# An S4 convolution and gated FFN, forward and backward: the order of the last forward convolution, the gates and the first backward convolution

## The chip, the cores and the metric

The kernel runs on one core of a Trainium2 chip. A time is device microseconds of one execution. Twelve runs of the kernel before gave a median of 740.47 us (737.26 to 746.09). One execution was also recorded by the profiler; every engine instruction, wait and transfer quoted below is of that one.

## What is computed

Input `x` is 2048 x 512 in bf16. A layer norm gives `xn`. Two branches read it. Branch A is a long causal convolution along the rows, one filter for each of the 512 channels, whose filters are built from complex exponentials (S4), plus a skip term. Branch B is a feed-forward net, `silu(xn @ w1) @ w2`, with w1 512 x 1792. The output multiplies A with a gate made of B:

```python
x = A_u
xn = _layernorm(x, axis=-1)
s = _A_ref(xn, A_A_re, A_A_im, A_B_re, A_B_im, A_C_re, A_C_im, A_log_dt, A_Dskip)
g = _silu(_B_ref(xn, B_w1, B_w2))
return x + s * g
```

The kernel returns this output and, for a given `grad_out`, the gradients with respect to x, the eight S4 parameters, w1 and w2. With o the result of the feed-forward net, the gradient that flows into branch A is `d s = grad_out * silu(o)`; the one that flows into branch B is `d o = grad_out * s * silu'(o)`.

## The kernel before, in words

The 2048 rows lie as 128 partitions x 16 row groups (t), the channels as 4 blocks of 128 (b). The work falls into stages.

**Forward.** `gen_tables` makes the filter of a block, `gen_conv_x` the spectrum of xn, `gen_conv_fwd` the convolution. A convolution is a transform in two TensorE steps with a transpose by DMA between them (`dft_fwd`, L276 to L300: matmuls L286, evacuations L287 by ScalarE, two transposes L288, matmuls L297 and L298, evacuations L299), a complex product on VectorE in two halves (`cplx_mul`, L323 to L337), and an inverse transform (`dft_inv`, L303 to L320: matmuls L310, evacuation L312, matmuls L319, and a `consume`). The evacuations have the line L44 or L45 in the profile, those of the helper `Evac` (A is ScalarE, D is VectorE). For the forward convolution `consume` adds the skip term and writes the block's result `S_b` (L518, L519). Beside this runs `gen_ffn_fwd` (hidden products L541, output products L558, result `ob`, stored to `Od`). At its end w1 and, later, w2 are turned on TensorE (L118), and each group of eight turned blocks is copied from PSUM back over the weight (tile W), by ScalarE and VectorE in turn (`evw`, pattern "AD", L1022).

**Gates.** `gen_gate_rows` (L569 to L604) goes through the rows in 8 chunks of two row groups. A chunk reads o, takes silu (tile g, three buffers, L593) and tanh (into the row store `do`, which the profile calls YD, L594) on ScalarE, writes `ds` on VectorE (L595), and makes d o with two operations on GpSimd (L597, L598) and four on VectorE (L599 to L603). L603 multiplies by the results S of blocks 0 to 2, loaded into a tile with two buffers (L589). `grad_out` is held whole in Gr, four loads of 512 KB (L576). The factor of block 3 comes last, when its convolution is done (L1101).

**Backward.** `gen_conv_bwd` needs all of `ds` for its first transform (L286 on ds), and then runs two inverse transforms for each block, one for the filter's gradient (dK) and one for the input's (du, L664 and L665). `gen_ffn_da` turns d o (doT), multiplies it with turned w2 (L886, ps_da), evacuates this on VectorE times the slope of silu (L888; the slope itself is two ScalarE and three VectorE operations for each half chunk, L875, L876 and L108 to L110), and multiplies with turned w1 (L897, ps_dx). `gen_out` makes the output. Then `gen_ssm_bwd` runs the gradient of the filter parameters, with `gen_ffn_da` and later the weight gradients (`gen_dw2`, `gen_dw1`) as TensorE work beside it; the weight gradient of w1 is the last.

**What sets the order.** The generators emit work in turns (`interleave`, `paced`, `woven`); the framework then orders the instructions of each engine by its own schedule, so that order of emission and order on an engine differ in places. [...]All plain loads and the DMA transposes of this part are issued by SyncE (SP), also in order: a load that waits for a buffer holds back all that stand behind it. PSUM tiles come from three pools: pf (3 buffers: feed-forward products, turned blocks), pc (2: transforms) and pt.

The part at issue, before:

```python
    interleave([gen_conv_fwd(k, 3), ffn, gates], [1, 3, 1])
```

then block 3's factor, the turning of w2, four steps of the backward convolution, and `paced(bwd, woven([ffb, out], [2, 1]), BR)`.

Of the kernel before, what the change touches and what calls it, by code (L numbers as in the profile page):

```python
# [10 lines left out]
ACT = mybir.ActivationFunctionType  # L11
ALU = mybir.AluOpType
F32 = mybir.dt.float32
BF16 = mybir.dt.bfloat16
# [3 lines left out]
P = 128  # L18
# [1 line left out]
PB = 18  # L20


BR, SR = 1.7, 0.5

E_EXP = [256 * i for i in range(1, 9)] + list(range(8)) + [258, 260, 262, 516, 772]
Y_EXP = [8 * j for j in range(1, 8)] + [64, 128, 192]
# [21 lines left out]
def interleave(gens, weights=None):  # L48
    gens = list(gens)
    weights = list(weights or [1] * len(gens))  # L50
    alive = [True] * len(gens)
    while any(alive):
        for i, g in enumerate(gens):
            if not alive[i]:
                continue
            for _ in range(weights[i]):
                try:
                    next(g)
                except StopIteration:
                    alive[i] = False  # L60
                    break
# [34 lines left out]
def paced(gen, other, rate):  # L96

    n = 0.0
    for _ in gen:
        n += rate  # L100
        while n >= 1:
            next(other, None)
            n -= 1
# [462 lines left out]

def gen_gate_rows(k, gp, lag):  # L569

    nc = k.nc
    TT = nc.vector.tensor_tensor
    last = k.T // 2
    Gr = gp.tile([P, k.T, k.D], BF16, name="Gr")
    for t in range(0, k.T, 4):
        nc.sync.dma_start(Gr[:, t:t + 4, :], k.g_v[:, t:t + 4, :])  # L576
    for c in range(last):
        while k.rows_done <= c or (c not in k.ob and k.rows_done < min(c + 1 + lag, last)):
            yield
        ts = slice(2 * c, 2 * c + 2)  # L580
        o = k.do[:, ts, :]
        src = o
        if c in k.ob:
            src = k.ob.pop(c)[:]
        else:
            nc.sync.dma_start(o, k.Od[:, ts, :])
        G = Gr[:, ts, :]
        S = gp.tile([P, 3, 2, P], BF16, name="S", tag="S", bufs=2)
        nc.sync.dma_start(S[:].rearrange("p b t d -> p b (t d)"), k.Sd[0:3, :, 256 * c:256 * c + 256].rearrange("b p n -> p b n"))  # L589
        if src is o:  # L590
            yield
        g = gp.tile([P, 2, k.D], BF16, name="g", tag="g", bufs=3)
        nc.scalar.activation(out=g[:], in_=src, func=ACT.Silu)  # L593
        nc.scalar.activation(out=o, in_=src, func=ACT.Tanh, scale=0.5)  # L594
        TT(out=k.ds[:, ts, :], in0=G, in1=g[:], op=ALU.mult)  # L595

        nc.gpsimd.tensor_scalar(out=o, in0=o, scalar1=-0.5, scalar2=0.5, op0=ALU.mult, op1=ALU.add)  # L597
        nc.gpsimd.tensor_scalar(out=g[:], in0=g[:], scalar1=1.0, scalar2=-1.0, op0=ALU.mult, op1=ALU.add)  # L598
        TT(out=o, in0=o, in1=g[:], op=ALU.mult)  # L599
        nc.vector.tensor_single_scalar(out=o, in_=o, scalar=1.0, op=ALU.add)  # L600
        TT(out=o, in0=o, in1=G, op=ALU.mult)
        o3 = o[:, :, 0:3 * P].rearrange("p t (b d) -> p b t d", b=3)
        TT(out=o3, in0=o3, in1=S[:], op=ALU.mult)  # L603
        yield  # L604


def gen_out(k, pool):
# [377 lines left out]
def kernel(ctx, tc, A_u, A_A_re, A_A_im, A_B_re, A_B_im, A_C_re, A_C_im, A_log_dt, A_Dskip, B_x, B_w1, B_w2, grad_out,  # L985
           out_0, out_1, out_2, out_3, out_4, out_5, out_6, out_7, out_8, out_9, out_10, out_11):
    nc = tc.nc
    k = KCtx()
    k.nc, k.tc = nc, tc
    k.outs = [out_0, out_1, out_2, out_3, out_4, out_5, out_6, out_7, out_8, out_9, out_10, out_11]  # L990
    L, D, F = A_u.shape[1], A_u.shape[2], B_w1.shape[1]
# [7 lines left out]
    def pool(name, side=None, es=ctx, **kw):  # L999
        kw.setdefault("bufs", 1)  # L1000
        return es.enter_context(tc.tile_pool(name=name, side=side, reuse_waits="tile", **kw))
# [17 lines left out]
    k.pc = ctx.enter_context(tc.tile_pool(name="pc", bufs=2, space=PSUM))  # L1019
    k.pt = ctx.enter_context(tc.tile_pool(name="pt", bufs=1, space=PSUM))  # L1020
    k.evk, k.evc, k.evf, k.evb, k.evv = (Evac(nc, "A") for _ in range(5))
    k.evx, k.evw = Evac(nc, "D"), Evac(nc, "AD")  # L1022

    k.st = nc.gpsimd.dma_start
    k.const = pool("const")
# [2 lines left out]
    es_f, es_x, es_t = (ctx.enter_context(ExitStack()) for _ in range(3))  # L1028
# [6 lines left out]
    with ExitStack() as es_s:  # L1035
# [6 lines left out]
        S = load_params(k, wp, 0, D, ("Ar", "Ai"))  # L1042
# [29 lines left out]
    def dft_pool(name, es, nbuf, base=None, **kw):  # L1072
        t = pool(name, es=es, **kw).tile
        return SimpleNamespace(tile=lambda shape, dt, name, tag: t(shape, dt, name=name, tag=tag, bufs=nbuf[tag]) if tag in nbuf
                               else base.tile(shape, dt, name=name, tag=tag))
# [14 lines left out]
    ffn = gen_ffn_fwd(k)  # L1090
    paced(chain(), ffn, 0.62)
    es_t.close()
    k.late = True
    k.ds = pool("ds", side="right", es=es_x).tile([P, 16, D], BF16, name="ds")
    es_g = es_x.enter_context(ExitStack())
    gates = gen_gate_rows(k, pool("gate", side="right", es=es_g), 1)

    interleave([gen_conv_fwd(k, 3), ffn, gates], [1, 3, 1])
    for t in (slice(0, 8), slice(8, 16)):
        last = k.do[:, t, 3 * P:4 * P]  # L1100
        nc.vector.tensor_tensor(out=last, in0=last, in1=k.S_b[:, t], op=ALU.mult)  # L1101
    es_f.close()
    es_g.close()
    base = dft_pool("dftb", es_x, {"cm2": 1, "xd": 1, "dD": 1, "w8b": 2}, k.dft, side="right")
    turn = itertools.cycle(["w8"] * 4 + ["w8b"] * 2)
    k.dftb = SimpleNamespace(tile=lambda shape, dt, name, tag: base.tile(shape, dt, name=name, tag=next(turn) if tag == "w8" else tag))
    da = pool("da", es=es_d)
    turned_in_place(k, k.W2, k.evw)
    bwd = gen_conv_bwd(k)
    out = gen_out(k, da)  # L1110
    for i in range(4):
        next(bwd)
    ffb = gen_ffn_da(k, da)
    paced(bwd, woven([ffb, out], [2, 1]), BR)
    es_x.close()
# [35 lines left out]
```

## Time and profile before

| what | value |
|---|---|
| median of 12 runs | 740.47 us |
| the profiled execution's own time | 740.77 us |
| its span, first to last instruction | 739.1 us |
| TensorE busy, of the span | 600.7 us (81%) |
| VectorE busy | 548.3 us (74%) |
| ScalarE busy | 506.6 us (69%) |
| GpSimd busy | 108.5 us (15%) |
| mean granted TensorE clock | 0.932 |
| chain that ended last: issue / VectorE / TensorE / DMA | 27% / 12% / 9% / 8% |

Time and span differ by 1.7 us, which lies around the program. A row of the table of windows gives, for a stretch of the span in us, how long each engine was busy in it, with the count of instructions, then the mean granted clock of TensorE (1.00 is full), the share of the DMA engines and their rate. A row of the timeline gives start and length of a merged run of instructions, its engine, line, operation and tiles; what stands in brackets is how long the engine had idled before it, and what released it. SPq and ACTq are the issuing queues.

### The profile page before, as it was taken

The page shows a single profiled execution, that of the slowest core. Times are in us where ns is not written, and L with a number is a line of the kernel's source. Part 1 is how long each engine was busy: PE and PEld are TensorE (multiplying, and loading weights), DVE is VectorE, ACT ScalarE, POOL GpSimd, SP SyncE. Part 2 cuts the span into 40 slices and gives each one's busy share as a digit, 9 for nine tenths or more (in the row PEclk, how much of TensorE's full clock was granted, in tenths as well). Part 3 has the DMA queues.
Part 4 walks back from the last instruction along what each step waited for, and adds up shares of the span by engine and source line. Part 5 has one row for each costly group of instructions (what it writes and reads, how often), then busy time and mean ns, then how long its engine had stood idle before and what let it go on. Part 6 is the DMA issues. An engine that isn't in the chain of part 4 may idle for free.

```text
span 739.1 us, 13979 instructions
## 1 busy us (share of the span) xinstructions
PE 600.7 (81%) x5459; PEld 432.0 (58%) x5500; DVE 548.3 (74%) x1086; ACT 506.6 (69%) x707; POOL 108.5 (15%) x180
## 2 busy tenths in 40 slices
PE   0667968869999955587989879978898978979995
PEld 0435645555675733454757657747576665756784
DVE  6969997869988759868698779747796677896000
ACT  7768759669799866857879587646846758882211
POOL 2172100000100034700000000000002003113210
PEclk9979989999999985789899989999999989999998
DMA  9877957679589776589988955789979999841782
GB/s 286 313 167 189 288 173 200 247 199 306 231 216 275 310 242 161 167 221 283 287 186 242 234 194 178 166 196 212 234 154 257 277 235 282 228 132 55 153 178 65
DMA packets 207042, 159.26 MB, mean 215 GB/s; under 512 B 129024, under 2 KB 185344, under 8 KB 203392
## 3 DMA queue, kind: packets, MB, share of 16 engines
q1 hardware_dynamic: 193856, 135.29, 69.3%
q0 software_dynamic: 6224, 18.10, 6.8%
q10 hardware_dynamic: 6896, 4.98, 2.1%
q8 instruction: 43, 0.70, 0.4%
q14 instruction: 23, 0.19, 0.1%
HBM read 65.14 MB, written 62.26 MB: 172 GB/s over the span
## 4 chain that ended last, share of the span: by engine, by line
issue 27%; DVE 12%; PE 9%; DMA 8%; POOL 4%; SPq 4%; ACT 2%; ACTq 0%; POOLq 0%; DVEq 0%
PE ps_da L886 2%; PE ps_dx L897 2%; DMA YT<-Yd 2%; DMA pd_l<-Pd 2%; SPq L718 2%; DVE sp_in L332 1%; SPq L346 1%; DVE Tp L739 1%; PE ps_v L729 1%; DMA out_dram<-go_x 1%; DMA Kd<-KE 1%; DVE sp_in L333 1%; DVE YD L599 1%; PE ps_i L310 1%; POOL out_dram L809 1%
## 5 line engine op out<-in xcount | busy, mean ns | idle before, releaser
L44 ACT CAST dA<-ps_s 128x1024 bf16<-128x1024 f32 x96 | 94.5, 1038 | 18.0 <-PE ps_s L298 9.6
L886 PE MATMUL ps_da<-doT,W 128*128 128x256 bf16 x448 | 62.7, 283 | 11.1 <-DVE dhT L888 7.1
L541 PE MATMUL ps_h<-XT,W 128*128 128x256 bf16 x448 | 62.5, 291 | 1.5 <-ACT hT L44 0.8
L310 PE MATMUL ps_i<-I,sp_in 128*128 128x256 bf16 x384 | 54.7, 288 | 8.5 <-DVE sp_in L333 4.2
L558 PE MATMUL ps_o<-W,aT 128*128 128x512 bf16 x209 | 54.5, 393 | 4.1 <-ACT aT L549 2.9
L886 PEld LDWEIGHTS <-W 128*128 128x128 bf16 x448 | 44.7, 102 | 21.8 <-issue 13.0
L739 DVE TENSOR_TENSOR Tp<-Vb,Eb 128x1344 bf16<-128x1344 bf16 x64 | 52.0, 853 | 6.9 <-issue 5.7
L44 ACT CAST dB<-ps_i 128x1024 bf16<-128x1024 f32 x48 | 47.1, 1019 | 12.9 <-PE ps_i L310 10.6
L897 PE MATMUL ps_dx<-W,dhT 128*128 128x512 bf16 x224 | 55.5, 388 | 0.5 <-ACT doT L44 0.5
L44 ACT CAST o<-ps_w 128x256 bf16<-128x256 f32 (+1 forms) x42 | 18.5, 442 | 50.9 <-PE ps_w L947 41.9
L541 PEld LDWEIGHTS <-W 128*128 128x128 bf16 x448 | 45.7, 104 | 12.7 <-issue 2.6
L929 PE MATMUL ps_w<-YD,a_tok 128*128 128x512 bf16 x210 | 51.3, 388 | 2.0 <-ACT o L44 1.2
L947 PE MATMUL ps_w<-dh_tok,xn 128*128 128x256 bf16 x448 | 50.5, 273 | 2.5 <-DMA dh_tok<-DHd 2.5
L310 PEld LDWEIGHTS <-sp_in 128*128 128x128 bf16 x384 | 37.7, 103 | 24.1 <-DVE sp_in L333 8.5
L888 DVE SCALAR_TENSOR_TENSOR dhT<-dhT,ps_da 128x512 bf16<-128x512 bf16 x56 | 37.5, 682 | 16.6 <-PE ps_da L886 16.2
L947 PEld LDWEIGHTS <-xn 128*128 128x128 bf16 x448 | 43.3, 98 | 8.9 <-issue 3.8
L44 ACT CAST Vb<-ps_v 128x672 bf16<-128x672 f32 x64 | 43.0, 730 | 6.7 <-PE ps_v L729 6.7
L286 PEld LDWEIGHTS <-TF 128*128 128x128 bf16 x384 | 27.0, 104 | 26.9 <-issue 15.3
L419 ACT ACTIVATE sn<-V 128x1024 bf16<-128x1024 int32 (+3 forms) x40 | 35.2, 899 | 8.8 <-DVE V L417 8.8
L729 PE MATMUL ps_v<-Gb,YT 128*128 128x168 bf16 x256 | 28.7, 243 | 14.3 <-ACT Vb L44 10.3
L297 PE MATMUL ps_s<-dB,F 128*128 128x512 bf16 x87 | 34.5, 404 | 6.9 <-DMA dB<-dA 4.2
L298 PE MATMUL ps_s<-dB,F 128*128 128x512 bf16 x95 | 36.9, 394 | 2.0 <-DMA dB<-dA 1.3
(223 smaller groups left out, 1383.5 us busy)
## 6 DMA issues: line engine op xcount, KB each, us to landing
Yd<-YD SPq DMA_DIRECT2D x8, 1024.0 KB, 5.6
sp_in<-Ud SPq DMA_DIRECT2D x8, 1024.0 KB, 7.8
h_in<-Hd SPq DMA_DIRECT2D x14, 512.0 KB, 5.1
Ed<-E SPq DMA_DIRECT2D x8, 672.0 KB, 5.1
Eb<-Ed SPq DMA_DIRECT2D x8, 672.0 KB, 5.4
Hd<-hT POOLq DMA_DIRECT2D x8, 512.0 KB, 6.1
Ud<-dA SPq DMA_DIRECT2D x4, 1024.0 KB, 9.8
KXd<-dA SPq DMA_DIRECT2D x4, 1024.0 KB, 6.3
```

The costliest lines, as they stand in the source:

```text
L44: return self.nc.scalar.copy(out=out, in_=in_)
L298: nc.tensor.matmul(out=ps[:, 4 * u:4 * u + 4], lhsT=F2[:, m1], rhs=B[:, 1, g0:g0 + 4, :], start=False, stop=True)
L310: nc.tensor.matmul(out=ps[:, g], lhsT=Y[:, c, g0 + g, :], rhs=k.I2[:, c].rearrange("p c m -> p (c m)"), start=(c == 0), stop=(c == 1))
L541: nc.tensor.matmul(out=ps[:, j], lhsT=k.W1[:, dk, ft * P:ft * P + P], rhs=XTv[:, :, dk, :], start=(dk == 0), stop=(dk == DK - 1))
L558: nc.tensor.matmul(out=ps[:], lhsT=aT[:, ft, t * P:t * P + P], rhs=k.W2[:, ft, :], start=(ft == 0), stop=(ft == FT - 1))
L729: nc.tensor.matmul(out=ps[:, u, 168 * c:168 * c + 168], lhsT=YT[:, c, q + u, :], rhs=Gb[:, q0 + q + u].rearrange("p w x -> p (w x)"), star ...
L739: k.nc.vector.tensor_tensor(out=Tp[:, c, :, r ^ c].rearrange("p e (q w) a -> p q w e a", w=2), in0=Vb[:, :, c].rearrange("p q w (e a) -> p ...
L886: nc.tensor.matmul(out=ps[:, j], lhsT=k.W2[:, ft, dk * P:dk * P + P], rhs=dTv[:, :, dk, :], start=(dk == 0), stop=(dk == DK - 1))
L888: nc.vector.scalar_tensor_tensor(out=dh[:, i0:i0 + 2, :], in0=dh[:, i0:i0 + 2, :], scalar=1.0, in1=ps[:], op0=ALU.add, op1=ALU.mult)
L897: nc.tensor.matmul(out=ps[:], lhsT=dhs[ft // 8][:, ft % 8, t * P:t * P + P], rhs=k.W1[:, :, ft * P:ft * P + P], start=(ft == 0), stop=(ft ...
L929: nc.tensor.matmul(out=ps[:], lhsT=at[:, t, :], rhs=k.do[:, t, :], start=(t == 0), stop=(t == k.T - 1))
L947: nc.tensor.matmul(out=ps[:], lhsT=k.xn[:, t, dk * P:dk * P + P], rhs=dh[:, t].rearrange("p j n -> p (j n)"), start=(t == 0), stop=(t == k ...
```

## The change

- The gates no longer run beside the last forward convolution in the order of emission. `gates` first emits the loads of three chunks; then `gen_conv_fwd(k, 3)` is emitted whole, with three steps of the feed-forward for each of its steps; then the gates, with the first backward convolution in turn with them.
- In a chunk, silu and d s come first, then tanh; d o of chunk c is emitted after d s of chunk c + 1.
- `grad_out` comes in chunks of 256 KB into a ring of four buffers instead of a whole tile.
- The backward convolution takes eight steps (EARLY) before the feed-forward backward is emitted, from the moment when all of d s is emitted; it was four. Its additional transform buffers are opened ahead of the gates.
- The turned weights are copied out of PSUM by VectorE alone (`evw` pattern "D").

```diff
-BR, SR = 1.7, 0.5
+BR, SR, EARLY = 1.7, 0.5, 8
...
-def gen_gate_rows(k, gp, lag):
+def gen_gate_rows(k, gp, ahead=3):
...
+    def load(c):
         ts = slice(2 * c, 2 * c + 2)
...
+        Gr[c] = gp.tile([P, 2, k.D], BF16, name="Gr", tag="Gr", bufs=4)
+        nc.sync.dma_start(Gr[c][:], k.g_v[:, ts, :])
+        if c < k.rows_done and c not in k.ob:
+            nc.sync.dma_start(k.do[:, ts, :], k.Od[:, ts, :])
+            held[c] = k.do[:, ts, :]
+
+    def d_s(c):
+        src = held.pop(c) if c in held else k.ob.pop(c)[:]
+        ts = slice(2 * c, 2 * c + 2)
         g = gp.tile([P, 2, k.D], BF16, name="g", tag="g", bufs=3)
         nc.scalar.activation(out=g[:], in_=src, func=ACT.Silu)
...
+        TT(out=k.ds[:, ts, :], in0=Gr[c][:], in1=g[:], op=ALU.mult)
+        nc.scalar.activation(out=k.do[:, ts, :], in_=src, func=ACT.Tanh, scale=0.5)
+        Sr[c] = gp.tile([P, 3, 2, P], BF16, name="S", tag="S", bufs=2)
...
+    for c in range(n):
...
+        g[c] = d_s(c)
+        k.ds_all = c == n - 1
+        yield
+        if c > 0:
+            d_o(c - 1, g.pop(c - 1))
+            yield
+        if c + ahead < n:
+            load(c + ahead)
+    d_o(n - 1, g.pop(n - 1))
...
-    k.evx, k.evw = Evac(nc, "D"), Evac(nc, "AD")
+    k.evx, k.evw = Evac(nc, "D"), Evac(nc, "D")
...
-    interleave([gen_conv_fwd(k, 3), ffn, gates], [1, 3, 1])
+    k.dfx = dft_pool("dfx", es_x, {"w8x": 2, "dD": 1}, k.dft, side="right")
+    turn = itertools.cycle(["w8", "w8x", "w8x", "w8", "w8", "w8"])
...
+    def early():
+        while not k.ds_all:
+            yield
+        for _ in range(EARLY):
+            next(bwd)
+            yield
+
+    next(gates)
+    paced(gen_conv_fwd(k, 3), ffn, 3)
+    interleave([gates, early()], [1, 1])
...
-    turn = itertools.cycle(["w8"] * 4 + ["w8b"] * 2)
...
+    k.dfx = dft_pool("dftb", es_x, {"cm2": 1, "xd": 1}, first, side="right")
...
-    for i in range(4):
-        next(bwd)
     ffb = gen_ffn_da(k, da)
     paced(bwd, woven([ffb, out], [2, 1]), BR)
```

The operations of d o, in `d_o`, are those of before.

## The prediction

> **What bounds the kernel now.** I read the page first: TensorE is busy 81% of the span, no other engine above 74%, and the chain that ended last spreads over all engines with no line above 2%. So no engine is the bound everywhere, and the question is which stretch is thin. The table of windows answers it:
>
> ```profile
> 270.00:280.00 10.00, 3.40 (x34) 2.95 (x32) 9.71 (x10) 5.01 (x6) 8.25 (x7) 0.65 0.50 186
> 280.00:290.00 10.00, 4.47 (x22) 2.55 (x23) 10.00 (x15) 5.38 (x7) 4.58 (x5) 0.50 0.85 189
> 290.00:300.00 10.00, 6.58 (x29) 3.27 (x28) 9.03 (x15) 9.14 (x10) 5.62 (x3) 0.67 0.56 206
> 300.00:310.00 10.00, 7.12 (x67) 5.46 (x66) 7.64 (x13) 9.47 (x10) 9.51 (x4) 0.82 0.62 184
> 310.00:320.00 10.00, 4.49 (x41) 4.16 (x41) 10.00 (x17) 6.66 (x7) 0.00 (x0) 0.66 0.39 83
> ...
> 440.00:475.00 35.00, 34.67 (x304) 24.88 (x303) 31.98 (x45) 25.00 (x26) 0.51 (x1) 1.00 0.53 167
> 475.00:490.00 15.00, 13.11 (x96) 8.46 (x95) 8.41 (x14) 7.67 (x6) 0.00 (x0) 1.00 0.84 150
> 490.00:510.00 20.00, 15.24 (x176) 12.85 (x175) 14.21 (x18) 9.29 (x15) 0.00 (x0) 0.91 0.91 227
> 510.00:530.00 20.00, 16.24 (x173) 12.49 (x172) 14.04 (x18) 17.61 (x21) 0.00 (x0) 0.91 1.11 224
> ```
>
> From 270 to 320 us TensorE (first pair) works 26.1 of 50 us at a clock of 0.50 to 0.82, while VectorE (third pair) is full in most rows: the gates. From 440 on TensorE is nearly full. The timeline shows how the gates hold block 3's convolution:
>
> ```profile
> 266.81 14.28 SPq L589 DMA_DIRECT2D S<-Sd  x3
> ...
> 270.22 2.73 DVE L595 TENSOR_TENSOR ds<-Gr,g 128x1024 bf16<-128x1024 bf16 x3 [8.11 <-DMA Gr<-in_grad_out_dram]
> ...
> 274.43 1.06 ACT L593 ACTIVATE g<-YD 128x1024 bf16<-128x1024 bf16 x1 [5.98 <-DVE YD L599]
> ...
> 281.19 4.83 SPq L288 DMA_TRANSPOSE dB<-dA  x2
> ...
> 310.58 1.21 DVE L519 TENSOR_TENSOR S_b<-ps_i,xd 128x1024 bf16<-128x1024 f32 x1
> ...
> 319.62 0.92 PE L886 MATMUL ps_da<-doT,W 128*128 128x256 bf16 x7 [2.02 <-ACT doT L44]
> ```
>
> VectorE waits 8.11 us for the gradient; so the fourth silu waits 5.98 us for a g buffer, and behind it stand the evacuations of the transform, whose matmuls were done at 269.6 (they come at 275.86). SP stands on the third S load until 281.1, and behind it stand the two transposes. Then VectorE mixes gate work into the product, whose first row (L330) comes at 293.66, and gets late to S_b. The feed-forward backward starts at 319.62.
>
> **The change, part by part.** The built order of each engine gives the sequence; durations are the trace's. Up to the inverse of block 2 (256.75) the two kernels agree.
>
> *Weights out of PSUM.* In the groups by form:
>
> ```profile
> L44 ACT COPY W<-pt_t 128x1024 bf16<-128x1024 bf16 x7 | 6.9, 1015 | 1.7 <-PE ps_i L319 1.7
> ...
> L45 DVE COPY W<-pt_t 128x1024 bf16<-128x1024 bf16 x7 | 4.8, 681 | 3.1 <-PE pt_t L118 3.1
> ```
>
> Seven copies leave ScalarE (6.9 us) and cost VectorE 4.8, about 0.6 each back to back, 4.2. [...] The rows have VectorE faster, so I take 4.2. The first four hide in VectorE's idle time from 252 to 258; the rest stand among the gates.
>
> *Gap, first half.* The new order has three Gr loads ahead of Kb's load, 0.75 MB against the 2 MB behind it before. Before, they took 5.3 us or more to land; issued at about 262 they land near 267 (bounds 265 and 270). VectorE then makes two d s, with weight copies between, 267 to 270; the weights' transposes stand ahead of Kb's matmuls, so these run at 270, later than 268.6 before. ScalarE has two ob evacuations, three silu and four tanh until 272 (nine rows of 0.6 to 1.06 us from 263.6) and no g wait in front of the transform; evacuations at 272 to 276 against 275.9 to 280.4. SP has only the fifth Gr load ahead of the transposes. This is the added wait: a ring of four, so it needs chunk 0's L601, about 273.5. The transposes stand behind it, and the first needs ScalarE until 274 anyhow: cost nothing, but each us by which that d o is later goes straight on. First transpose 274 against 281.2: gain 7.
>
> *Gap, second half.* Transposes land 4.7 us after issue and 2.4 apart: second transform at 279 and 281 (285.9 and 288.25 before). VectorE's product starts at 284.5 (293.66): before it stand four d s that had to wait for Gr chunk 4, three d o and the copies. Two halves with gate work between, 4.7 and 5.4 us, end at 294.6 (303.3). Between there and S_b stand two d s, xd, and six d o operations, 4.9 us: S_b at 299.5 (310.58). Then 5.5 us to block 3's factor, and evacuations of the first backward transform ahead of doT: ps_da at 309. Gain **10.6**. Bounds: 4 if Gr lands at 270 and GpSimd (16 operations of 1.04 to 1.47 us) is late, 14 if the waits are shorter.
>
> *Early backward.* In the new order only 24 ps_da follow, for their evacuation needs the slope, and the slope stands on ScalarE behind eight evacuations of the backward transforms, a go_g and on VectorE behind most of two complex products: first evacuation near 335, against 322.7. The backward block's two spectra (1 MB each) go onto SP just ahead of its transposes, at 0.53 us of issue each, as one of them did before: nothing. Until 335 TensorE has (0.216 us a matmul of 512 columns, from 28 L897 in 6.21 us back to back, and less in proportion) 24 x 0.108 + 16 x 0.216 + 32 x 0.054 + 32 x 0.108 + 32 x 0.054 = 12.7 of 26 us. That looks like a new hole, [...]; by the row of 320 to 330, which was already 89% busy, nothing. The chain there is ScalarE and VectorE, so I charge 1.
>
> But this stretch brings the convolutions forward: the first inverse ends near 336 against 352.8. The backward convolutions are VectorE's: after the second L1101, up to the last du, it has 122.5 us in the old order (16 products' steps, 35 L888, ten slopes; back to back 0.60 for the 0.68 us rows and 1.14 for 1.22) in 153.5 us, 317.5 to 471, a share of 0.80. In the new order it has 115.9 us (28 L888, nine slopes). From 307 at the same share: 145 us, last du at 452. **Gain at that point 19.** Bounds 9 (share 0.75) and 32 (0.88; the last row above had 0.91).
>
> *What is left over.* Less feed-forward lies before that point: 224 ps_da and 90 ps_dx against 279 and 112. So 55 x 0.108 + 22 x 0.216 = **10.7 us** of TensorE work goes to the later stages. TensorE has it in the last 84.5 us, otherwise nearly full. Bounds 6 (the 19% idle of 475 to 530 takes some) and 15 (that mixture of filter gradients and feed-forward is itself thin, 44.6 of 55 us, and becomes longer).
>
> Sum: 19 - 10.7 - 1 = 7.3 off the profiled execution's 740.77 (span 739.1 and 1.7 around it), which is 733.5; the median is 0.3 below that execution, so **733.0**. Bounds from both unknowns: +2 slower to 22 faster.
>
> **Rivals.** (1) As above, 728 to 738: chance 0.48. (2) VectorE runs the backward convolutions densely, because they are two products ahead and nothing of the feed-forward's stands in between: share 0.85, 136 us, last du at 443, gain 28, less 11.7: 16, so 724. For: 0.91 at 440 to 475. Against: the inverse transforms wait for evacuations and pc has two buffers. Chance 0.20. (3) Other side: the feed-forward starves. Its slope stands behind the transforms on ScalarE, its evacuations wait, and its pf buffers hold TensorE. If the last du comes later than about 459, the gain of 12 no longer pays the 10.7 and the 1; at a share of 0.74 it is 464, gain 7, so 745. For: the 12.7 of 26 us. Against: what was starved runs later as filler. Chance 0.18. (4) It does not do what it says: the fifth Gr load sits on SP ahead of the transposes and waits for d o. With GpSimd's rows at 1.47 and VectorE's at 1.5 where both work, d o of chunk 0 is at 278, the gain in the gap 4, and 19 becomes 12: 740. Chance 0.14.
>
> **Numbers.** A measurement of this kernel can tell about 0.3%, 2.2 us, from no change. Faster by more: 0.48 + 0.20, and a little from (4): 0.69. Within: 0.13. Slower: 0.18. The range leaves out the denser half of (2) and the worse half of (3): 722 to 744.
>
> **What would show it.** First transpose of block 3 at 274 (wrong if over 278: then Gr or the ring holds SP); S_b at 300; ps_da at 309; the first L888's counterpart at 335 with TensorE below 60% from 310 to 335; last du at 452 (over 459: slower); the stage of filter gradients as long as before; the weight gradients' tail longer by some 9 us. The prediction is wrong if VectorE's share in the backward convolutions isn't near 0.8, or if that tail doesn't grow.

## The result: 1.1% slower, and where the time stands in the profile after

The changed kernel took 746.08 us, the median of 12 runs (742.56 to 749.88), beside 738.68 us (49 runs, 731.12 to 746.09) for the kernel before: **1.0112 times**, 95% interval 1.0087 to 1.0137. The ratios leave out executions more than 1.5% above the fastest of their kernel: 6 of the 49 here, so that the ratio is not quite that of the two medians (1.0100), and 26 of 49 in one comparison below, EARLY 8 without overlap, for which the medians of all executions are given too. Run again later, beside three other kernels, the changed kernel had 1.016 [1.0116, 1.0203]. The profiled execution took 744.11 us (span 742.4). Single executions of one kernel lie up to 1.5% from their median, so a few us between two profiles carry nothing alone; verdicts below rest on the ratios, and the profiles say where to look.

The table of windows of the changed kernel, columns as in the prediction's (TensorE, weight loads, VectorE, ScalarE, GpSimd, then the clock). Behind the gates the lines of the changed kernel have numbers 21 higher: L888 is L909 here.

```profile
270.00:280.00 10.00, 2.59 (x36) 2.21 (x33) 10.00 (x14) 8.07 (x10) 5.33 (x6) 0.71 0.50 95
280.00:290.00 10.00, 6.95 (x18) 2.37 (x19) 9.25 (x14) 6.53 (x8) 6.52 (x5) 0.61 0.92 264
290.00:300.00 10.00, 5.00 (x22) 2.65 (x23) 10.00 (x14) 4.21 (x5) 2.40 (x2) 0.56 0.45 161
300.00:310.00 10.00, 7.80 (x67) 6.75 (x66) 8.97 (x14) 3.23 (x4) 3.90 (x2) 0.59 0.18 46
310.00:320.00 10.00, 4.05 (x31) 2.48 (x28) 4.03 (x8) 3.57 (x4) 0.00 (x0) 0.75 1.07 279
320.00:330.00 10.00, 7.40 (x49) 4.39 (x49) 3.95 (x6) 5.91 (x7) 0.00 (x0) 0.91 0.98 259
330.00:345.00 15.00, 10.60 (x82) 8.21 (x80) 15.00 (x23) 12.79 (x14) 0.50 (x1) 0.68 0.70 175
```

and two rows of the kernel before:

```profile
320.00:330.00 10.00, 8.92 (x60) 5.95 (x60) 5.63 (x9) 3.32 (x4) 0.00 (x0) 0.83 0.93 258
330.00:345.00 15.00, 13.82 (x107) 8.71 (x106) 13.21 (x19) 11.69 (x11) 0.60 (x1) 1.00 1.11 249
```

From 270 to 310 VectorE is busy 38.2 of 40 us (36.4 before). New are the rows from 310 to 330: VectorE works 8.0 of 20 us, ScalarE 9.5, TensorE 11.5. No computing engine is the bound there; all of them wait. (The share of the DMA engines is high there, 1.07 and 0.98, but so it was before, 0.93 and 1.11 from 320 to 345.) The timeline says for what:

```profile
274.44 5.86 SPq L288 DMA_TRANSPOSE dB<-dA  x2
...
291.24 16.38 SPq L592 DMA_DIRECT2D S<-Sd  x3
...
305.54 1.23 DVE L519 TENSOR_TENSOR S_b<-ps_i,xd 128x1024 bf16<-128x1024 f32 x1
...
310.84 4.32 SPq L288 DMA_TRANSPOSE dB<-dA  x1
...
313.62 0.38 PE L907 MATMUL ps_da<-doT,W 128*128 128x256 bf16 x2 [1.86 <-ACT doT L44]
...
315.83 5.31 SPq L288 DMA_TRANSPOSE dB<-dA  x1
...
322.88 0.38 SPq L895 DMA_DIRECT2D slope<-Hd  x1
...
324.09 1.93 ACT L44 CAST dA<-ps_s 128x1024 bf16<-128x1024 f32 x2 [10.53 <-PE ps_s L298]
...
332.27 1.98 ACT L896 ACTIVATE dhT<-slope 128x2048 bf16<-128x2048 bf16 x1
...
341.97 1.27 DVE L909 SCALAR_TENSOR_TENSOR dhT<-dhT,ps_da 128x512 bf16<-128x512 bf16 x2
```

and in the kernel before:

```profile
300.32 1.09 SPq L874 DMA_DIRECT2D slope<-Hd  x2
303.80 0.36 SPq L589 DMA_DIRECT2D S<-Sd  x1
...
322.68 0.69 DVE L888 SCALAR_TENSOR_TENSOR dhT<-dhT,ps_da 128x512 bf16<-128x512 bf16 x1 [1.14 <-PE ps_da L886]
```

The first transpose of block 3 comes at 274.44 as forecast (281.19 before), and ps_da at 313.62 (319.62 before). But SP then stands on the last S loads for 16.38 us, until 307.6, and only behind the backward transform's transposes does it issue the first load of the slope, at 322.88. The kernel before issued it at 300.32, ahead of its last S load. Meanwhile ScalarE stands idle for 10.53 us, until the second transpose has let TensorE finish the transform; it has no slope to work on. The first evacuation of ps_da that is multiplied with a slope (L909) comes at 341.97, the kernel before's at 322.68.

Two figures sum up each profile: when the last du begins, and how long the program lasts after it. Before: 469.8 and 269.3. After: 459.1 and 283.3. The changed kernel is 10.7 us ahead at the last du, and loses 14.0 behind it.

### The profile page after: what moved, and what is told of

Read it like the earlier page. It is cut to its first block, busy times and chain, and to the rows that moved or that the text cites. A ratio compares the mean times of both kernels' runs of the same rounds, so it can differ in the third digit from the quotient of the medians.

```text
span 742.4 us, 13992 instructions
## 1 busy us (share of the span) xinstructions
PE 600.6 (81%) x5460; PEld 431.9 (58%) x5500; DVE 553.3 (75%) x1093; ACT 500.1 (67%) x700; POOL 100.4 (14%) x180
## 4 chain that ended last, share of the span: by engine, by line
issue 24%; PE 14%; DVE 12%; DMA 6%; ACT 4%; SPq 3%; POOL 3%; POOLq 0%; DVEq 0%; ACTq 0%
PE ps_w L950 3%; PE ps_dx L918 2%; SPq L739 2%; PE ps_v L750 2%; DVE sp_in L332 1%; PE ps_da L907 1%; PE psS L772 1%; DMA slope<-Hd 1%; PE psS L776 1%; DVE dhT L909 1%; DMA go_g<-Od 1%; DMA pd_l<-Pd 1%; SPq L346 1%; ACT Vb L44 1%; DVE cm L331 1%
## 5 line engine op out<-in xcount | busy, mean ns | idle before, releaser
L310 PE MATMUL ps_i<-I,sp_in 128*128 128x256 bf16 x384 | 57.2, 299 | 18.4 <-DVE sp_in L333 10.4
L907 PE MATMUL ps_da<-doT,W 128*128 128x256 bf16 x448 | 60.7, 281 | 7.0 <-ACT pd_s L44 2.9
L918 PE MATMUL ps_dx<-W,dhT 128*128 128x512 bf16 x224 | 53.6, 379 | 1.8 <-DVE dhT L909 1.8
L909 DVE SCALAR_TENSOR_TENSOR dhT<-dhT,ps_da 128x512 bf16<-128x512 bf16 x56 | 37.4, 681 | 17.1 <-PE ps_da L907 16.6
L297 PE MATMUL ps_s<-dB,F 128*128 128x512 bf16 x87 | 34.3, 401 | 16.3 <-DMA dB<-dA 11.5
L286 PEld LDWEIGHTS <-TF 128*128 128x128 bf16 x384 | 25.1, 100 | 25.0 <-issue 12.9
L447 PEld LDWEIGHTS <-YD 128*128 128x128 bf16 x512 | 24.9, 103 | 23.3 <-DVE YD L434 12.7
```

Source lines behind the costliest of these rows:

```text
L310: nc.tensor.matmul(out=ps[:, g], lhsT=Y[:, c, g0 + g, :], rhs=k.I2[:, c].rearrange("p c m -> p (c m)"), start=(c == 0), stop=(c == 1))
L907: nc.tensor.matmul(out=ps[:, j], lhsT=k.W2[:, ft, dk * P:dk * P + P], rhs=dTv[:, :, dk, :], start=(dk == 0), stop=(dk == DK - 1))
L909: nc.vector.scalar_tensor_tensor(out=dh[:, i0:i0 + 2, :], in0=dh[:, i0:i0 + 2, :], scalar=1.0, in1=ps[:], op0=ALU.add, op1=ALU.mult)
L918: nc.tensor.matmul(out=ps[:], lhsT=dhs[ft // 8][:, ft % 8, t * P:t * P + P], rhs=k.W1[:, :, ft * P:ft * P + P], start=(ft == 0), stop=(ft ...
```

## The experiments

Two ideas lay behind the first four. *Left-over*: BR paces the feed-forward backward by the steps of the backward convolution, so steps taken ahead (EARLY) leave feed-forward work for later. *Gates*: VectorE is overloaded in the gap. In all counts below "ps_da" and "ps_dx" are single matmuls of that kind in TensorE's order ahead of the last inverse transform (where the recorded expectations say groups, single matmuls are meant). Of 448 and 224 the kernel before has 279 and 112, the changed one 224 and 90.

### Undoing one part at a time

**Four early steps.** `EARLY = 8` to `4` in the changed kernel.

> The changed kernel with four early steps of the backward convolution in place of eight. In its order 256 ps_da and 112 ps_dx stand before the last inverse (changed: 224 and 90; before: 279 and 112). Theory L (left-over: the gap gains about 6 us, but the convolutions run ahead and 10.7 us of feed-forward is paid at the end): 2.5 us left over, so 5 to 8 us less than the changed kernel, ratio to before about 0.99 to 1.00. Theory G (the gates: VectorE overloaded by weight copies and GpSimd, the order of the first convolution) and theory S (SP stands on the S loads): as slow as the changed kernel, 1.01.

Measured: 1.0124 [1.0094, 1.0154]. 256 and 112 matmuls, and no gain.

**Pacing the left-over back.** `BR = 1.7` to `2.1` in the changed kernel; 279 and 112 as before.

> The changed kernel with eight early steps, but the feed-forward backward paced at 2.1 of its steps for each convolution step in place of 1.7, which brings 279 ps_da and 112 ps_dx before the last inverse as in the kernel before. Theory L: no left-over, the hole at the start of the backward part stays: 4 to 8 us less than the changed kernel, ratio 0.99 to 1.00. Theories G and S: 1.01.

Measured: 1.0158 [1.0135, 1.0181]. Left-over work can't be the only cause.

**Copies of the weights.** `evw` back to "AD" in the changed kernel, and the converse, "D" in the kernel before.

> The changed kernel with the turned weights copied by ScalarE and VectorE in turn, as before. Theory G: VectorE loses 4.2 us of copies among the gates, 3 to 5 us less than the changed kernel, ratio 1.005 to 1.007. Theories L and S: within 2 us of the changed kernel, ratio 1.009 to 1.014.

> The kernel before with one edit: all fourteen weight copies by VectorE. By the prediction's rows ScalarE loses 6.9 us and VectorE gains 4.2 us where it bounds, ratio 0.998 to 1.003 under every theory of the loss; outside of that the copies are a cause of their own.

Measured: 1.0148 [1.0120, 1.0176] and 1.0021 [0.9995, 1.0048]. The copies are not the cause; alone they are at most half a per cent, and perhaps nothing.

**Eight steps in the kernel before.** `for i in range(4): next(bwd)` to `range(8)`; 224 and 84 matmuls.

> The kernel before with eight steps of the backward convolution ahead of the feed-forward backward in place of four; gates and first convolution as before. In its order 224 ps_da and 84 ps_dx stand before the last inverse, but the first ps_da and the first inverse stand where they stood. Theory L: 12 us of TensorE work go to the end without the gap's gain: 5 to 10 us slower than before, ratio 1.007 to 1.013. Theories G and S: within 2 us of before, 1.00.

Measured: 1.0105 [1.0058, 1.0152]. Steps ahead at the old pacing cost a per cent with none of the other edits. So the steps ahead, or the work that they leave over, cost something, and there is something else in the changed kernel.

### The new gates alone, and the early steps away

The new idea, H: in the changed kernel the backward part opens with a hole, a stretch in which the engines wait. The next two kernels both keep the new gates and the weight copies. In the second only `EARLY` is 0. In the first all of the backward arrangement is that of the kernel before:

```diff
-    k.dfx = dft_pool("dfx", es_x, {"w8x": 2, "dD": 1}, k.dft, side="right")
...
-    interleave([gates, early()], [1, 1])
+    run(gates)
...
+    base = dft_pool("dftb", es_x, {"cm2": 1, "xd": 1, "dD": 1, "w8b": 2}, k.dft, side="right")
+    turn = itertools.cycle(["w8"] * 4 + ["w8b"] * 2)
...
+    for i in range(4):
+        next(bwd)
```

> The new gates, the last forward convolution ahead of them and the weight copies on VectorE, but no early backward: the backward convolutions begin as in the kernel before, after the gates' pool has been closed, with its four steps ahead of the feed-forward. Theory H (the early backward opens a hole: its transposes and product stand alone while the feed-forward's loads and silu come behind them on SP and ScalarE): the loss goes away, first ps_da near 314, the stage from there to the last du 148 to 151 us, tail 85 us, ratio 0.990 to 0.998. Theory G (what costs is the gates in one stretch without feed-forward work, with GpSimd beside VectorE): the loss stays, ratio 1.005 to 1.012, and the stage to the last du is again 155 us or more for as much TensorE work as before. Theory L (left-over work alone): counts before the last inverse are as before, so ratio 0.99 to 0.995.

> The changed kernel with EARLY at 0: the backward convolutions stay in the changed kernel's buffers, but their first step is taken only when the feed-forward is paced with them, so the feed-forward's first loads and silu are emitted from the start in between. As many ps_da groups (280) and ps_dx groups (125) as before or more come ahead of the last inverse. Theory H: no hole, the stage from the first ps_da to the last du has TensorE over 0.88 busy, ratio 0.99 to 1.00. Theory G: like the early-4 run, ratio 1.008 to 1.015. Theory L: 0.99 to 0.995.

> The changed kernel itself, run beside the other three on one chip, so that each of them has its own comparison with it. All theories: 1.009 to 1.014 times the kernel before.

Measured on one chip: gates alone 0.9976 [0.9953, 1.0000], EARLY 0 in the changed kernel 1.0145 [1.0100, 1.0189], the changed kernel 1.016 [1.0116, 1.0203]. The gates were innocent: ps_da starts 4.2 us earlier (315.4) and the rest is as before. But H fell in the form I gave it: without any early step, and with as much feed-forward work emitted among the convolutions as before, the hole was still there (its windows stand below). SP's timeline of the gates-alone kernel shows what differs:

```profile
292.12 0.37 SPq L592 DMA_DIRECT2D S<-Sd  x1
...
294.46 0.50 SPq L895 DMA_DIRECT2D slope<-Hd  x1
299.02 0.37 SPq L592 DMA_DIRECT2D S<-Sd  x1
299.43 0.49 SPq L895 DMA_DIRECT2D slope<-Hd  x1
307.96 0.36 SPq L592 DMA_DIRECT2D S<-Sd  x1
```

and of the changed kernel with EARLY 0:

```profile
293.21 16.20 SPq L592 DMA_DIRECT2D S<-Sd  x3
...
312.00 5.08 SPq L288 DMA_TRANSPOSE dB<-dA  x1
...
325.17 0.38 SPq L895 DMA_DIRECT2D slope<-Hd  x1
```

With the old arrangement the framework had put two slope loads between the last S loads, at 294 and 299; ScalarE then made the first slopes from 304.10 on, while VectorE did gates until 314. Now they come at 325. The generators emit them late in both.

### A pool that lies 288 bytes over another

The addresses that the program was built with say why. The feed-forward backward's pool (`da`: slopes, dhT, doT, the tiles of `gen_out`, pd_s) takes bytes 83968 to 117760 of a partition, where two pools of the forward part lay. In the kernel before the gate pool begins at 125920, and with the gates alone at 134112. In the changed kernel the early transform buffers (16.25 kB) lie outside the gate pool, push it down, and it begins at **117472**: its first Gr buffer lies under the last 288 bytes of `da`, in tile pd_s. The idea is that what is loaded into `da` is then ordered behind the gates' work.

Four kernels on one chip test it. The first three are the changed kernel with 288 bytes less of constants below `da`, so that it ends at 117472 (EARLY 8, 4 and 0):

```diff
-        k.zero = k.const.tile([P, P], BF16, name="zero")
-        nc.gpsimd.memset(k.zero[:], 0.0)
-        k.onesf = k.const.tile([P, 1], F32, name="onesf")
-        nc.gpsimd.memset(k.onesf[:], 1.0)
-        k.ecst = k.const.tile([P, NE + len(Y_EXP)], F32, name="ecst")
+        k.ecst = k.const.tile([P, NE + len(Y_EXP) + 1], F32, name="ecst")
+        k.onesf = k.ecst[:, NE + len(Y_EXP):]
+        nc.gpsimd.memset(k.onesf, 1.0)
...
+    k.zero = sb.tile([P, P], BF16, name="zero")
+    k.nc.gpsimd.memset(k.zero[:], 0.0)
```

The fourth does the opposite to the gates-alone kernel:

```diff
+    pad = gp.tile([P, 8448], BF16, name="pad")
+    nc.gpsimd.memset(pad[:, 0:8], 0.0)
```

> The changed kernel, EARLY 8, with 288 bytes per partition less of constants below the feed-forward's pool (a zero tile made later, a one kept in a spare column), so that this pool ends at 117472 where the gate pool begins, and no longer lies 288 bytes over it. Nothing else differs. Theory O (the overlap makes the feed-forward's pool wait for the gates, which puts its first loads of slopes behind the last S loads and the early transposes on SP): the first slope load goes from 323 us to about 295, its silu and tanh fall into the gates' stretch, the hole between 314 and 341 is gone, and the stage from the first ps_da to the last du drops from 145.5 to about 138, as in the kernel before with 8 early steps; span 734 to 737. O with L (the left-over work still costs what the 8 early steps cost in the kernel before, 1 per cent): ratio 1.003 to 1.008. O alone, with early steps free: 0.990 to 0.998. Without O: 1.009 to 1.016 as before.

> The kernel of the same call without the overlap, with EARLY at 4. 249 ps_da groups come before the last inverse, 25 more than with 8. Theory O with L: ratio 0.994 to 1.000, stage to the last du near 148, tail near 85. O alone: as with 8. Without O: 1.009 to 1.015, as the early-4 run with the overlap had (1.0124).

> The kernel without the overlap, with EARLY at 0 (280 ps_da groups and 126 ps_dx groups before the last inverse). Theory O: ratio 0.993 to 1.000 where the same kernel with the overlap had 1.0145, first slope load near 295. Without O: 1.010 to 1.018.

> The converse: the kernel with the new gates and the old backward arrangement (0.9976), with an unused tile of 16.5 kB put in the gate pool, so that the gate pool begins at 117216, 544 bytes inside the feed-forward's pool. No instruction of the work differs but their order: the slope loads come behind the last S loads and the transposes, 28 fewer ps_da groups before the last inverse. Theory O: first slope load near 325, stage to the last du 155 us or more, ratio 1.007 to 1.016. Without O: 0.995 to 1.000.

Measured: EARLY 8 **1.0117** [1.0086, 1.0148], and 1.0072 by the medians of all executions (744.68 and 739.39 us); EARLY 4 **1.0113** [1.0067, 1.0159], six executions; EARLY 0 **1.0015** [0.9994, 1.0036]; gates with pad **1.0093** [1.0063, 1.0123]. In all four the first slope load moved as expected: to 294.5, 294.7 and 298.2 us without the overlap, to 322.8 with it. Two adjacent windows of the EARLY 0 kernel, with the overlap:

```profile
315.00:330.00 15.00, 8.15 (x36) 4.49 (x37) 1.84 (x4) 3.30 (x5) 0.00 (x0) 0.78 1.08 250
330.00:345.00 15.00, 7.98 (x59) 6.05 (x59) 14.17 (x21) 13.90 (x12) 0.60 (x1) 0.67 0.69 177
```

and without it:

```profile
315.00:330.00 15.00, 10.97 (x73) 7.22 (x71) 10.82 (x18) 8.41 (x9) 0.89 (x1) 0.77 1.01 254
330.00:345.00 15.00, 12.94 (x112) 9.03 (x110) 13.95 (x21) 13.05 (x14) 0.54 (x1) 1.00 1.01 244
```

TensorE works 16.1 us with the overlap and 23.9 without. So where little is left over the overlap is worth 1.3% (1.0145 against 1.0015, measured on two chips) and, put in, 1.2% (0.9976 to 1.0093, two chips as well; the pad run also has 28 fewer ps_da ahead, so up to 28 x 0.108 = 3.0 us of it may be left-over work, an estimate: in the kernel before one ps_da took 0.27 us and fifteen in a row 1.80, 0.109 for each further one). With early steps the picture is less clear. EARLY 4 stayed as slow as it was with the overlap (1.0124). For EARLY 8 it depends on how the executions are taken: 1.0117 is no gain on the 1.0112 to 1.016 of the changed kernel, while 1.0072 would be most of what the forecast called "O with L" (1.003 to 1.008). The changed kernel was not run beside its version without overlap. What this chip does show is the price of early steps once the overlap is out: medians of 744.68 us for EARLY 8 and 748.31 for EARLY 4, against 739.37 for EARLY 0. With the overlap in, on the other chip, EARLY 8 and EARLY 0 were alike (745.27 and 745.15). In the profile the hole was filled (with EARLY 8 TensorE works 23.5 us in these two windows), and yet the stage to the last du took 144.1 us, not the expected 138. So there is a second cause.

### Left-over work alone, and both causes out

Four edits of numbers: `BR = 1.7` to `1.6` in the gates-alone kernel; the kernels without overlap with `BR = 2.1` and EARLY 8, and with `BR = 1.9` and EARLY 4; and the gates-alone kernel without its `for i in range(4): next(bwd)`.

> The kernel of new gates and old backward arrangement (0.9976) with one number changed, BR from 1.7 to 1.6: 224 ps_da matmuls instead of 279 come before the last inverse, 55 times 0.108 or 5.9 us of TensorE work less. No early step, no overlap. Theory T: left-over work alone makes the loss, 5 to 9 us, ratio 1.004 to 1.012. Theory E: 0.996 to 1.000.

> The changed kernel without the 288 bytes of overlap and with BR at 2.1 instead of 1.7: all of its edits are in, its early backward of 8 steps too, but both suspected causes are out. 280 ps_da matmuls and 115 ps_dx matmuls come before the last inverse, as before (279 and 112). Theory T (two causes, each enough for the whole loss: the overlap, and feed-forward work left over behind the backward convolutions): ratio 0.990 to 1.001, where either edit alone gave 1.0117 and 1.0158. Theory E (the early steps themselves cost, whatever is left over): 1.008 to 1.013.

> The same with EARLY at 4 and BR at 1.9 (280 and 119 matmuls before the last inverse). Theory T: ratio 0.990 to 1.001, where the early-4 kernel without the overlap, with 249 and 112, had 1.0113. Theory E: 1.006 to 1.012.

> The same kernel at BR 1.7 without its four backward steps ahead of the feed-forward: 280 ps_da and 128 ps_dx matmuls before the last inverse. Theory T: nothing left over, so 0.995 to 1.001. Theory E: as much or faster, 0.990 to 0.998.

Measured on one chip: left-over alone (gates alone, BR 1.6) **1.0049** [1.0025, 1.0074]; EARLY 8 without overlap, BR 2.1 **1.0068** [1.0043, 1.0092]; EARLY 4 without overlap, BR 1.9 **1.0050** [1.0027, 1.0073]; gates alone with no step ahead **0.9934** [0.9909, 0.9960], faster than both kernels. The first lies where theory T had it. The two with both causes out lie between the theories, nearer to E; the last is within E's range and outside T's nominal 0.995.

Left-over work costs by itself: 0.9976 to 1.0049 is 0.73% of 735 us, 5.4 us (two chips; by the two intervals 0.4 to 1.1%). The windows from the first ps_da to the last du, on to the first and to the last ps_v (the matmuls of the filters' gradient), and to the end show how. Gates alone:

```profile
315.40:464.60 149.20, 132.57 (x1110) 94.45 (x1114) 123.19 (x176) 111.65 (x119) 7.36 (x12) 0.94 0.81 228
464.60:488.20 23.60, 19.96 (x143) 12.55 (x141) 13.17 (x20) 11.31 (x9) 0.00 (x0) 1.00 0.93 194
488.20:646.40 158.20, 139.78 (x1439) 105.03 (x1450) 123.56 (x293) 110.38 (x168) 16.16 (x30) 0.96 0.96 237
646.40:730.80 84.40, 70.27 (x659) 56.69 (x659) 23.02 (x76) 24.45 (x54) 15.96 (x27) 0.97 0.46 109
```

The same with BR 1.6:

```profile
315.40:455.70 140.30, 123.94 (x1051) 89.17 (x1055) 116.19 (x167) 107.59 (x117) 6.54 (x12) 0.95 0.85 234
455.70:481.30 25.60, 20.83 (x160) 15.02 (x158) 13.69 (x21) 8.22 (x7) 0.00 (x0) 0.93 0.77 189
481.30:646.50 165.20, 146.96 (x1452) 109.14 (x1462) 123.88 (x285) 112.84 (x164) 14.85 (x28) 0.93 0.90 222
646.50:736.40 89.90, 76.19 (x690) 60.86 (x691) 29.09 (x93) 29.51 (x63) 17.30 (x30) 0.96 0.49 121
```

The stage of the backward convolutions (first row) is 8.9 us shorter, since VectorE has 7.0 us less to do there; the three rows behind it are 14.5 us longer in sum. TensorE's busy time falls by 8.6 us in the first and grows by 14.0 in the others, where the granted clock is also lower in the execution with BR 1.6. Times the clock of its row, TensorE's busy time is about 125 and 118 us in the first row and 222 and 229 in the others (an estimate from these rows): the same 7 us leave and arrive. So the surplus goes with the lower clock, and no run shows whether the edit brings that about.

With both causes out, the eight early steps still stand at 1.0068. The rest was sought in the buffers: without any early step the new arrangement had 1.0015 and the old one 0.9934. One line, the order in which the 8 kB buffers are handed out, went back to that of before:

```diff
-    turn = itertools.cycle(["w8", "w8x", "w8x", "w8", "w8", "w8"])
+    turn = itertools.cycle(["w8"] * 4 + ["w8x"] * 2)
```

> The changed kernel without overlap and with EARLY 0 (1.0015), with one line edited: the 8 kB buffers are handed out in the order of the kernel before (four of the old ring, then the two new ones). The first K spectrum then waits for a buffer of the last forward convolution and is loaded behind the two transposes on SP instead of ahead of them; the order on SP up to 350 us, and the 280 and 128 matmuls before the last inverse, are those of the kernel with the old backward arrangement and no steps ahead (0.9934). Theory R (the order in which the buffers are handed out, which puts the 1 MB load of K ahead of the transposes, is the third part of the loss): ratio 0.990 to 0.997, first transpose near 312 us and 3.0 us on SP as there, not 315.9 and 4.4. Theory P (it is where the pools lie, or the 288 bytes of constants moved): 1.000 to 1.004.

> The changed kernel with EARLY 8, without overlap, with BR 2.1 (1.0068), and with the old order of the buffers. What is left of the loss beside 0.9934 is then the price of the eight early steps. Theory R: 0.996 to 1.002, the early steps costing some 0.4 per cent, as four steps ahead cost between 0.9934 and 0.9976. Theory P: 1.004 to 1.009.

Measured: 0.9983 [0.9957, 1.0009] without early steps, 1.0140 [1.0098, 1.0183] with eight. The first lies between the two theories and decides for neither. The second is against both: the old order made the kernel with early steps slower, not faster. The order of the buffers is no separate part of the loss that could be added up.

All together, without overlap first (last du and the time behind it from one profiled execution each; the ratios come from several chips, each against the kernel before beside it):

| kernel | overlap | ps_da, ps_dx ahead | last du, rest (us) | ratio |
|---|---|---|---|---|
| before | no | 279, 112 | 469.8, 269.3 | 1 |
| gates alone, 0 steps | no | 280, 128 | 465.6, 263.3 | 0.9934 |
| gates alone, 4 steps | no | 279, 112 | 464.6, 266.2 | 0.9976 |
| early 0, old turn | no | 280, 128 | 468.1, 264.5 | 0.9983 |
| early 0 | no | 280, 126 | 468.3, 271.2 | 1.0015 |
| gates alone, BR 1.6 | no | 224, 110 | 455.7, 280.7 | 1.0049 |
| early 4, BR 1.9 | no | 280, 119 | 467.0, 271.4 | 1.0050 |
| early 8, BR 2.1 | no | 280, 115 | 470.7, 270.2 | 1.0068 |
| before, 8 steps | no | 224, 84 | 454.9, 282.2 | 1.0105 |
| early 4 | no | 249, 112 | 467.8, 279.5 | 1.0113 |
| early 8 | no | 224, 88 | 459.7, 284.7 | 1.0117 (medians 1.0072) |
| early 8, BR 2.1, old turn | no | 280, 115 | 472.8, 271.5 | 1.0140 |
| gates alone, pad | yes | 251, 112 | 472.1, 272.5 | 1.0093 |
| early 8 (the change) | yes | 224, 90 | 459.1, 283.3 | 1.0112 |
| early 4 | yes | 256, 112 | 476.4, 266.6 | 1.0124 |
| early 0 | yes | 280, 125 | 474.7, 269.1 | 1.0145 |
| early 8, BR 2.1 | yes | 279, 112 | 475.7, 267.4 | 1.0158 |

What is shown: the new gates cost nothing; the overlap costs 1.2 to 1.3% where little else is left over; left-over work costs 0.7% alone. What is not settled: why the two do not add in the changed kernel (1.0112 to 1.016 with both, 1.0072 to 1.0117 without the overlap, 1.0158 without left-over work, 1.0068 without both), and what the 0.7% is that eight early steps still cost when both are out. Steps ahead of the feed-forward may cost in the old arrangement too: 0.4% for four (0.9934 to 0.9976, on two chips), hardly more than the noise.

The profiles give a hint to the open part, not a cause. From the first ps_da to the last du VectorE was busy 0.82 to 0.83 of the time in the kernel before, with four or eight steps, in the three gates-alone kernels without pad, and in the two kernels with EARLY 0 without overlap. With early steps in the new buffers and no overlap it was 0.78 to 0.82 in five kernels, 0.80 with EARLY 8: there VectorE waits more.

## Why the prediction was wrong

Forecast 733.0 us against 740.47, 0.990 times; measured 746.08, 1.0112 times, beyond the range's end of 744. (Two of its sums are slightly off: the terms of TensorE's hole add to 13.0 us, not 12.7, and 740.77 - 7.3 - 0.3 is 733.2.) Most of the miss lies in two terms, the second half of the gap and what is left over; the early backward was misread. Step by step:

- **Weights out of PSUM**: direction right, small. Fourteen VectorE copies took 9.0 us, 0.64 each, and the experiment on the kernel before leaves -0.05 to +0.48% for the move. VectorE's own row was the right price; ScalarE's copies of the same shape had taken 1.015 us each in the kernel before, so VectorE was the cheaper engine here.
- **Gap, first half**: right. First transpose 274.44 for 274; second transform 279.9 for 279. Rival (4), the fifth Gr load in SP's way, did not occur: it was issued at 274.05.
- **Gap, second half**: the step that failed by most. ps_da came 6.0 us earlier, not 10.6. The product began at 287.0 for 284.5, its halves ended at 299.3 for 294.6, S_b came at 305.5 for 299.5. The term that was too small is VectorE's rows beside GpSimd, which I had costed near their price alone: five of them between 282.87 and 303.00 took 1.51 or 1.52 us where 0.68 is the price alone (the row at 277.03), 4.2 us more in sum, and two waits for GpSimd were 1.7 (the last section shows such rows). That is a reading of the timeline; no experiment took GpSimd out. So block 3's factor was done at 313.5 us, not at 307.
- **Early backward**: the reading failed, at a small price in this sum. I put the late slope down to its place on ScalarE behind eight evacuations, and there it does stand (L896, 332.27). But it was put there because its load had gone from ahead of the last S load on SP to behind the transposes, 22.6 us later than before (322.88 for 300.32), and that by the place of a pool. The rule that I laid on myself, to count each queue that a step is moved past, I applied to the spectrum loads and not to the slopes, which the diff does not touch. The first evacuation came at 341.97 for 335. I saw the hole on TensorE (12.7 of 26 us forecast; measured, 22.1 of the 35 us from 310 to 345, against 27.2 before) and charged 1 us, an estimate; VectorE's share, below, makes it about 3, and the stage of EARLY 8 without overlap, with the hole filled, was 1.4 us shorter (144.1 for 145.5). The two spectra, put at nothing, may not have been free either: with one just ahead of each, the two backward transposes held SP for 4.32 and 5.31 us, where it was 2.80 and 5.54 before, with one ahead of the second alone. The clock in the hole was 0.75, 0.91 and 0.68 (0.66, 0.83 and 1.00 in the same three rows before); what that cost is shown by no run.
- **VectorE's share in the backward convolutions**: the number came true, 0.80, partly by luck. My 0.80 for the kernel before was 122.5 us of reckoned work in 153.5; the trace counts 125.85 us there, 0.82. So the share did fall, from 0.82 to 0.80 in the two rows below the list. At the first row's share 116.3 us of VectorE's work would have taken 142.5 us, not 145.5 (an estimate). The last du ended at 460.3 and not 452, a gain of 10.7 us against 19. Of the 8.3 us missing, 6.5 were there when the stretch began (313.5 for 307), and 1.8 came in it. Rival (3) named this point, "over 459: slower", and its time of 745 came true, but by other terms: it had the feed-forward starve VectorE to a share of 0.74 and the last du at 464. It had 0.18.
- **What is left over**: mis-sized, 10.7 us (11.7 with the early backward's 1) for 14.0. In the changed kernel the stage of the filter gradients is 3.5 us longer (165.3 for 161.8; forecast, as long as before) and the tail 11.2 (95.7 for 84.5; "some 9" forecast); a short stage ahead of them is 0.7 shorter. I had held both at TensorE's rate. Nor was TensorE "nearly full" from 440 on: my own rows have it at 87, 76 and 81% from 475 to 530. The left-over kernel above shows 14.5 us for 8.6 us of TensorE's time moved.

From the first ps_da to the last du, in the kernel before and in the changed one:

```profile
319.60:469.80 150.20, 133.66 (x1110) 95.75 (x1114) 122.55 (x175) 111.74 (x119) 7.34 (x12) 0.93 0.80 226
313.60:459.10 145.50, 122.91 (x1021) 87.91 (x1025) 116.31 (x166) 108.52 (x116) 6.51 (x12) 0.93 0.79 227
```

So the sum 19 - 10.7 - 1 became 10.7 - 14.0, 3.3 us slower between the two profiled executions (744.11 and 740.77); the medians differ by 7.4, since the execution before lies 2.1 above its median and the one after 2.0 below. The form of the argument, a gain up to the last du set against what comes back behind it, held; its terms were wrong by 8.3 and 2.3 us, both to the hopeful side. The sum accounts for the two executions; why the kernel stays slow when the overlap and the left-over work are both taken out of it is open. The deeper error is that BR was taken as given: at a fixed pacing, convolutions that finished 10.7 us earlier did not end the program earlier. They handed their feed-forward work on, and in these profiles the stages that received it grew by more than the first one shrank (14.5 us against 8.9 with BR 1.6).

## What to carry to other kernels

Opening a buffer earlier can push another pool down until it touches a third that reuses freed memory; then loads that had been moved ahead for free wait, as the first slope load did here (issued at 322.9 us with the overlap, 294.5 without), and neither the diff nor the count of instructions shows it. Compare the addresses of pools, and the place of every load on its queue, also of those that the diff does not name. And where filler work is paced by the steps of a chain, a faster or earlier chain can just move the filler, here 55 ps_da and 22 ps_dx: look at the stage that receives it before the gain is booked.

## What the chip showed beside

One VectorE operation, L600 with two bf16 inputs of 128x1024, took 0.68 us at 277.03 with no GpSimd operation beside it, 1.51 at 282.87 and 303.00, where a GpSimd operation had begun 0.07 us before, and 2.53 at 269.12, where one had begun 0.08 us before and a second began in its course. In the changed kernel's timeline:

```profile
269.04 1.05 POOL L598 TENSOR_SCALAR YD<-YD 128x1024 bf16<-128x1024 bf16 x1
269.12 2.53 DVE L600 TENSOR_TENSOR YD<-YD,g 128x1024 bf16<-128x1024 bf16 x1
270.05 1.05 POOL L599 TENSOR_SCALAR g<-g 128x1024 bf16<-128x1024 bf16 x1
...
277.03 0.68 DVE L600 TENSOR_TENSOR YD<-YD,g 128x1024 bf16<-128x1024 bf16 x1
...
282.80 1.04 POOL L599 TENSOR_SCALAR g<-g 128x1024 bf16<-128x1024 bf16 x1
282.87 1.51 DVE L600 TENSOR_TENSOR YD<-YD,g 128x1024 bf16<-128x1024 bf16 x1 [0.75 <-POOL YD L598]
...
300.07 3.90 POOL L599 TENSOR_SCALAR g<-g 128x1024 bf16<-128x1024 bf16 x2 [4.70 <-DVE ds L589]
300.44 0.68 DVE L600 TENSOR_TENSOR YD<-YD,g 128x1024 bf16<-128x1024 bf16 x1
...
303.00 1.51 DVE L600 TENSOR_TENSOR YD<-YD,g 128x1024 bf16<-128x1024 bf16 x1 [0.94 <-POOL g L599]
```

The 2.53 us row ends 0.55 us after GpSimd's second operation, the first 1.51 us row 0.54 us after the one beside it, as if VectorE had waited for them and then run. That is a reading of the times; no row names the cause. It was not always VectorE's operation that ran longer: at 300.44 the same operation took 0.68 us beside a GpSimd operation, the first of the two from 300.07 on, that took 2.89. By the rows of 1.51 a GpSimd operation of the gates can cost VectorE some 0.83 us (an estimate), and in the gap, where VectorE is busy 38.2 of 40 us, that can go straight onto the path. It is no new cost of the change: added up over the gates, such rows are 8.7 us above their price alone before and 8.6 after (an estimate from the two timelines).

In these profiles the backward part's first two transposes by DMA held SP for longer where a 1 MB spectrum load stood just ahead: in the kernel before 2.80 us without one and 5.54 with one; in the fastest kernel (gates alone, no step ahead) 3.00 and 3.03, without; 4.41 with and 2.97 without (new gates, EARLY 0, no overlap); 5.83 and 5.57, both with (EARLY 8, no overlap). No experiment gave this alone a price.
